# The reciprocal roots of the first two batches on ScalarE and VectorE instead of GpSimd, in a fused attention and Fourier-mixing kernel

## The chip, the core and the metric

The kernel runs on one core of a Trainium2 chip. The core has TensorE (matrix products, the profile's PE, with its weight loads as PEld), VectorE (DVE), ScalarE (ACT), GpSimd (POOL) and SyncE (SP), which here issues every data transfer. Each engine takes its instructions in the order in which they stand in its own queue, and waits for what they need. The metric is device microseconds for one execution, and lower is better. A difference of 0.2%, some 4.3 us here, is about what a measurement of this kernel can tell from no change.

## What is computed

The reference is an attention block, its heads joined to rows of 768, and behind it a mixing block. For 8 batches, 12 heads, 448 tokens and a head dimension of 64:

```python
def rmsnorm(x, g):
    rms = np.sqrt(np.mean(x * x, axis=-1, keepdims=True) + 1e-06)
    return x / rms * g
q_n, k_n = rmsnorm(q, g_q), rmsnorm(k, g_k)
scores = (1 / np.sqrt(64)) * np.matmul(q_n, k_n.transpose(0, 1, 3, 2))
attn = softmax(scores)                      # max taken off, sum + 1e-9
x = heads_joined(np.matmul(attn, v))        # [8, 448, 768]
u = x + real(fft(fft(x, axis=1), axis=2))
un = (u - mean(u)) / np.sqrt(var(u) + 1e-06)
out = u + np.maximum(un @ w_ch1, 0) @ w_ch2 # 768 -> 3072 -> 768
```

The change touches one thing in it: the factor 1/rms of every token and head, for queries and keys, in batches 0 and 1 of the 8.

## The kernel before

**Stages of a batch.** `aux(b)` holds everything of batch b ahead of the feed-forward part: `attention` (pair by pair of heads), then `spectral` (the Fourier mixing as matrix products, the sums u and the second norm). `ffn(b, ...)` holds the feed-forward part: 24 "up" steps of 18 matmuls each (line 910) and 36 "down" steps of 12 each (line 931). `merge` interleaves `ffn(b)` with `aux(b+1)` by a ratio of costs, so that TensorE has feed-forward matmuls to do while ScalarE and VectorE work on the next batch's attention. Ahead of `ffn(0)` nothing of the kind is there: `aux(0)` runs by itself, with the first 14 steps of `aux(1)` mixed into its spectral part.

**A pair of heads.** `load_pair` brings queries and keys of two heads to the tile `raw` (112 tokens by 1024) and the values to `v`. `norm_pair` squares them into `qkn`, sums each row of 64 (`V.tensor_reduce` to `ss`, 112x16), scales the sums, takes the power -1/2, and multiplies `raw` by it into `qkn`. `transpose_pair` turns `qkn` on TensorE (tiles `qk`, line 327), splits the result in two parts for two matmul passes (`QT`, `KD`, and `rounded`, which holds the keys' low parts), `softmax_pair` makes the scores `S` (line 375), their row minimum `mn` on VectorE and the exponential `P` on ScalarE, and `value_pair` turns `P` (tiles `rem` and `pt`) into `T` and `R` and multiplies by the values (`av`). In batches 0 and 1 the division by the row sums is made later, on the result (`divide_pair`: `sums`, `rs`, `rt`, `xT`).

**The norm's engines.** In batches 0 and 1 (`b < EARLY`) the squares are made on ScalarE, in the others on GpSimd. The reduction and the scaling are VectorE's, the power is GpSimd's in all batches: one `tensor_tensor` with `ALU.pow` of `ss` (112x16) against a tile of -0.5.

**The weights.** They come as 64-bit numbers. In the first sweep each block is loaded (`dblw`, in the early part `dblw1e` and `dblw2e`), converted and stored back to memory for the later sweeps. `convert` (lines 711 to 731) takes two instructions of ScalarE, three of VectorE, one addition on GpSimd (line 728, tile `magw`), a cast on ScalarE and a subtraction on VectorE (`w`). Loaded blocks share two buffers, so that a load waits for the GpSimd addition of the block two before it.

**The order.** The program is written in the order of these generators, and a scheduler that works with modelled costs then sets the order of each engine's queue. Each generator's step yields a cost. Buffers are few and shared by tag. So a change in one place gives another order in many queues around it. All transfers are issued from SyncE's one queue.

Of the kernel before, what the change touches and what calls it, by code (L numbers as in the profile page):

```python
# [11 lines left out]
F32 = mybir.dt.float32  # L12
# [3 lines left out]
AF = mybir.ActivationFunctionType  # L16
ALU = mybir.AluOpType
# [5 lines left out]
C = 112  # L23
# [19 lines left out]
EARLY = 2  # L43
# [46 lines left out]
def spectral_block(ctx, tc, q, k, v, g_q, g_k, w1, w2, d1, d2, out, nb=B):  # L90
    nc = tc.nc
# [3 lines left out]
    sb = ctx.enter_context(tc.tile_pool(name="sb", bufs=2))  # L95
# [23 lines left out]
    V, A, G = Recorded(nc.vector), Recorded(nc.scalar), Recorded(nc.gpsimd)  # L119
# [59 lines left out]
    nhalf = cpool.tile([128, 16], F32, name="nhalf")  # L179
# [7 lines left out]
    def load_gains():  # L187
        for i, g in enumerate((g_q, g_k)):
            for h in range(2):
                nc.sync.dma_start(  # L190
                    gains[64 * h : 64 * h + 64, i : i + 1],
                    g.rearrange("(d o) -> d o", o=1),
                )
        V.scalar_tensor_tensor(
            out=gneg, in0=gneg, scalar=-(D**-0.5), in1=gains[:, 1:], op0=ALU.mult,
            op1=ALU.mult,
        )
# [49 lines left out]
    def norm_pair(b, p):  # L247
        raw, vt = loaded.pop((b, p))
        qk = sb.tile([C, 2, NC, 2, D], F32, tag="qk", name=f"qkn{b}_{p}", bufs=1)
        sq = qk.rearrange("t i c h d -> t (i c h) d")  # L250
        flat = raw.rearrange("t i h c d -> t (i h c) d")
        nth = b * NPAIR + p
        if b < EARLY:
            A.activation(sq, flat, AF.Square)
        else:
            G.tensor_tensor(out=sq, in0=flat, in1=flat, op=ALU.mult)
        ss = sb.tile([C, 16], F32, tag="ss", name=f"ss{b}_{p}")
        V.tensor_reduce(ss, sq, axis=AX.X, op=ALU.add)
        V.tensor_scalar(
            out=ss, in0=ss, scalar1=1.0 / D, scalar2=EPS, op0=ALU.mult, op1=ALU.add  # L260
        )
        G.tensor_tensor(out=ss, in0=ss, in1=nhalf[:C], op=ALU.pow)
        for i in range(2):
            V.tensor_tensor(
                out=qk[:, i].rearrange("t c h d -> t h c d"),
                in0=raw[:, i],
                in1=ss[:, 8 * i : 8 * i + 8]
                .rearrange("t (h c) -> t h c", h=2)[:, :, :, None]
                .broadcast_to([C, 2, NC, D]),
                op=ALU.mult,  # L270
            )
        if plain(b, p):
            return qk, vt
        vhl = sb.tile([128, 4, 4, D], F32R, tag="vhl", name=f"vhl{b}_{p}", bufs=1)
        A.copy(vhl[:, :, ::3], vt)
        V.tensor_tensor(
            out=vhl[:, :, 1:3], in0=vt, in1=vhl[:, :, ::3], op=ALU.subtract
        )
        return qk, vhl
# [3 lines left out]
    def plain(b, p):  # L283


        return b * NPAIR + p in PLAIN_PAIRS
# [6 lines left out]
    def transpose_pair(b, p):  # L293

        if b >= nb or (b, p) in ready:
            return
        load_pair(b, p)
        qk, vhl = norm_pair(b, p)
        load_pair(*next_pair(b, p))
        yield 0  # L300
# [665 lines left out]
    def warm():  # L966
# [4 lines left out]
        for _ in range(8):  # L971
            nc.tensor.matmul(o, ident, w, start=True, stop=True)

    load_gains()
    load_pair(0, 0)
    warm()
# [41 lines left out]
```

## Time and profile before

| | us |
|---|---|
| median of 3 runs (2168.72 to 2171.92) | 2169.73 |
| the profiled execution | 2168.48 |
| its span, first to last instruction | 2166.7 |
| TensorE busy with matmuls in the span | 2082.8 (96%) |
| VectorE, ScalarE, GpSimd busy | 1556.7, 1055.5, 342.6 |

Times in a timeline or chain row are counted from the start of the span: start, duration, engine, line, operation, tiles written and read, and in brackets how long the engine stood idle before and what ended that. Line 113 is the helper that records ScalarE's, VectorE's and GpSimd's instructions, so the tile names tell them apart. A row of waits gives the sum, the number of times and the longest. A row of a table by stretch gives, for each engine, its busy time and in brackets its instructions; the column behind POOL is TensorE's granted clock as a share of full speed.

### The profile page before, as it was taken

Reading aid. Unit: us, or ns where it says so; the run is one execution under the profiler, and the core shown is the slowest. Engines: PE = TensorE matmul, PEld = TensorE weight load, DVE = VectorE, ACT = ScalarE, POOL = GpSimd, SP = SyncE. Lnnn points to the kernel's source line nnn. Section 1 sums busy time; section 2 is a strip of 40 time slices with the busy share of each in tenths; the row PEclk is TensorE's granted clock in tenths of the full one; section 3 lists DMA queues with packets and bytes.
Section 4 is the critical chain, followed back from the end, with each engine's and each line's share of the span. In section 5 each row is a group of like instructions: output and inputs, shape, how many; then the busy total and the mean of one; then the engine's idle time right before and its main releaser. Section 6 shows DMA issues by size and latency. Waiting matters only on the chain.

```text
span 2166.7 us, 31325 instructions
## 1 busy us (share of the span) xinstructions
PE 2082.8 (96%) x11224; PEld 1857.7 (86%) x11224; DVE 1556.7 (72%) x3003; ACT 1055.5 (49%) x2258; POOL 342.6 (16%) x196
## 2 busy tenths in 40 slices
PE   7877999899999999999999999999999999999997
PEld 4556777789999999999999999999999999998997
DVE  7888878978785788758786688857787588753122
ACT  7967866455552555435552455425553455422100
POOL 3324434221110111001110111101110011000000
PEclk8988999999999999999999999999999999999999
DMA  5647777677565855667565765658556675449665
GB/s 167 185 131 266 243 262 243 204 236 224 162 174 184 244 173 165 186 200 218 165 174 178 224 194 172 179 183 241 166 173 190 188 219 165 157 157 287 214 211 138
DMA packets 298301, 424.74 MB, mean 196 GB/s; under 512 B 186609, under 2 KB 224482, under 8 KB 298146
## 3 DMA queue, kind: packets, MB, share of 16 engines
q1 hardware_dynamic: 298146, 422.74, 63.8%
q8 instruction: 89, 1.46, 0.3%
q14 instruction: 66, 0.54, 0.1%
HBM read 362.50 MB, written 65.27 MB: 197 GB/s over the span
## 4 chain that ended last, share of the span: by engine, by line
PE 79%; DVE 6%; DMA 6%; ACT 4%; issue 2%; POOL 1%; SPq 0%; DVEq 0%; POOLq 0%; ACTq 0%
PE o L931 29%; PE h L910 28%; PE S L375 6%; PE av L485 4%; DMA dblw<-w 4%; PE pt L473 4%; PE y L590 2%; PE qk L327 1%; DMA w<-w 1%; ACT P L113 1%; PE oT L876 1%; POOL magw L728 1%; PE x L622 1%; DVE qkn L113 1%; PE un L822 1%
## 5 line engine op out<-in xcount | busy, mean ns | idle before, releaser
L931 PE MATMUL o<-hs,w 128*128 128x448 f32 x3456 | 794.8, 372 | 7.0 <-DMA w<-w 2.6
L910 PE MATMUL h<-unT,w 128*128 128x448 f32 x3456 | 778.7, 370 | 4.1 <-ACT unT L113 1.6
L931 PEld LDWEIGHTS o<-hs,w 128*128 128x128 f32 x3456 | 639.5, 189 | 64.5 <-DMA w<-w 4.9
L910 PEld LDWEIGHTS h<-unT,w 128*128 128x128 f32 x3456 | 639.2, 188 | 58.2 <-issue 2.4
L113 ACT ACTIVATE P<-S,mn 112x448 f32<-112x448 f32 x384 | 243.7, 636 | 197.9 <-DVE mn L113 183.9
L113 ACT ACTIVATE hs<-h 128x448 fp32r<-128x448 f32 x192 | 104.3, 543 | 311.6 <-PE h L910 309.7
L113 DVE TENSOR_REDUCE mn<-S 112x1 f32<-112x448 f32 x384 | 233.7, 618 | 28.1 <-PE S L375 25.5
L113 DVE SCALAR_TENSOR_TENSOR hs<-h,hs 128x448 fp32r<-128x448 f32 x192 | 119.4, 622 | 149.2 <-ACT hs L113 147.4
L113 DVE TENSOR_TENSOR acc<-o,acc 128x448 f32<-128x448 f32 x240 | 148.7, 620 | 96.8 <-PE o L931 94.2
L113 POOL TENSOR_TENSOR qkn<-raw 112x1024 f32<-112x1024 f32 x36 | 68.6, 1906 | 697.8 <-PE qk L327 354.8
L113 POOL TENSOR_TENSOR ss<-ss,nhalf 112x16 f32<-112x16 f32 x48 | 144.7, 3014 | 183.2 <-DVE ss L113 164.8
L375 PE MATMUL S<-KD,QT 128*112 128x448 f32 x384 | 152.3, 399 | 16.3 <-ACT KD L113 11.1
L113 ACT CAST T<-pt 128x448 fp32r<-128x448 f32 x216 | 113.1, 533 | 99.8 <-PE pt L473 98.5
L485 PE MATMUL av<-T,vhl 128*128 128x448 f32 x432 | 153.4, 383 | 0.0
L113 DVE TENSOR_TENSOR T<-pt,T 128x448 fp32r<-128x448 f32 x216 | 131.6, 618 | 26.6 <-ACT T L113 25.6
L375 PE MATMUL S<-rounded,QT 128*112 128x448 f32 x384 | 143.2, 375 | 0.4 <-DMA v<-v 0.4
L113 DVE TENSOR_SCALAR P<-P,sm 112x448 f32<-112x448 f32 x288 | 122.5, 463 | 4.1
L473 PE MATMUL pt<-ident,P 112*128 112x112 f32 x864 | 121.8, 259 | 0.0
L473 PEld LDWEIGHTS pt<-ident,P 112*128 112x128 f32 x864 | 102.6, 140 | 15.5
L728 POOL TENSOR_TENSOR magw<-magw,dblw 128x512 uint32<-128x512 uint32 (+1 forms) x46 | 75.4, 1639 | 172.9 <-DVE magw L724 103.1
L113 POOL TENSOR_TENSOR rstd<-st,nhalf 112x1 f32<-112x1 f32 (+2 forms) x32 | 19.6, 612 | 492.3 <-DVE st L113 489.2
L375 PEld LDWEIGHTS S<-KD,QT 128*112 128x112 f32 x384 | 69.2, 181 | 27.9 <-ACT KD L113 13.7
(117 smaller groups left out, 2521.9 us busy)
## 6 DMA issues: line engine op xcount, KB each, us to landing
w<-w SPq DMA_DIRECT2D x192, 768.0 KB, 4.5
w<-w SPq DMA_DIRECT2D x288, 512.0 KB, 4.3
dblw<-w SPq DMA_DIRECT2D x28, 512.0 KB, 5.1
dblw<-w SPq DMA_DIRECT2D x18, 768.0 KB, 5.9
raw<-q SPq DMA_DIRECT2D x96, 112.0 KB, 3.3
raw<-k SPq DMA_DIRECT2D x96, 112.0 KB, 3.7
v<-v SPq DMA_DIRECT2D x96, 96.0 KB, 3.1
u_dram<-u SPq DMA_DIRECT2D x24, 336.0 KB, 3.4
```

Source lines behind the costliest of these rows:

```text
L113: ins = emit(*args, **kwargs)
L327: nc.tensor.transpose(pt[:, c * C : (c + 1) * C], qk[:, i, c].rearrange("t h d -> t (h d)"), ident[:C, :C],)
L375: ins = nc.tensor.matmul(s_, QT[:, h, cs], K[:, h], start=step == 0, stop=step == 1)
L473: nc.tensor.transpose(pt[:, c * C : (c + 1) * C], Pc[c][:, 512 * h + j * 128 : 512 * h + (j + 1) * 128], ident[:C, :C],)
L485: nc.tensor.matmul(av[:, :S], lv, T[:, i], start=(j == 0 and i == 0), stop=False)
L590: nc.tensor.matmul(o, src[:, par, t0 : t0 + n], D1[:, ri, par, cols], start=i != 1, stop=i != 0,)
L622: nc.tensor.transpose(xp[:n, i * 128 : (i + 1) * 128], src[:, 3 * half + i], ident)
L728: behind(nc.gpsimd.tensor_tensor(out=bits, in0=bits, in1=low, op=ALU.add))
L822: nc.tensor.transpose(pt[:, OFFS[i] : OFFS[i] + LENS[i]], uns[i][:, p * 128 : (p + 1) * 128], ident[: LENS[i], : LENS[i]],)
L876: nc.tensor.transpose(op[:n, j * 128 : (j + 1) * 128], accs[b][:, 3 * half + j, t0 : t0 + n], ident,)
L910: pace(nc.tensor.matmul(o, w[:, a, c], unT[c][:, z], start=n == 0, stop=n == 17))
L931: pace(nc.tensor.matmul(o, w[:, a, f], hs[4 * g + f][:, z], start=n == 0, stop=n == 11))
```

## The change

In batches 0 and 1 the power -1/2 of `ss` is no longer taken on GpSimd. ScalarE takes the natural logarithm into a new small tile `y`, then the exponential of -1/2 times that, and the square of the result into a second tile `z`. VectorE makes one Newton step with two instructions: z becomes -1/2 z ss, and ss becomes (z + 3/2) y. Batches 2 to 7 keep GpSimd's power. At the program's start ScalarE's table set that holds both logarithm and exponential is asked for explicitly, ahead of the first loads.

```diff
@@ norm_pair
-        G.tensor_tensor(out=ss, in0=ss, in1=nhalf[:C], op=ALU.pow)
+        if b < EARLY:
+            y, z = (
+                sb.tile([C, 16], F32, tag=tag, name=f"{tag}{b}_{p}") for tag in "yz"
+            )
+            A.activation(y, ss, AF.Ln)
+            A.activation(y, y, AF.Exp, scale=-0.5)
+            A.activation(z, y, AF.Square)
+            V.scalar_tensor_tensor(
+                out=z, in0=z, scalar=-0.5, in1=ss, op0=ALU.mult, op1=ALU.mult
+            )
+            V.scalar_tensor_tensor(
+                out=ss, in0=z, scalar=1.5, in1=y, op0=ALU.add, op1=ALU.mult
+            )
+        else:
+            G.tensor_tensor(out=ss, in0=ss, in1=nhalf[:C], op=ALU.pow)
@@ at the program's start
+    nc.scalar.preload_act_table_set("natural_log_exp_and_others")
     load_gains()
     load_pair(0, 0)
     warm()
```

Twelve GpSimd instructions go (of 48 such powers), and 36 ScalarE and 24 VectorE instructions come. The built program holds one table load in both versions. The scheduler gives another order in all queues up to about the end of `ffn(0)`; behind that, TensorE's last 5092 of 5980 rows stand as before.

Three places show how the queues move. The first is the start of ScalarE's queue. The number behind a tile's name is a buffer's; `qkn_0` is the square of the first pair, and each row's wait is by a semaphore name: DMAHW for a transfer, DVE, PE, Activation for an engine. Before:

```order
L113 ACT_TABLE_LOAD [waits DMAHW2_49,DMAHW3_49,DMAHW1_49]
L113 ACTIVATE qkn_0_136<-raw_0_113 112x1024 [waits DMAHW0_49]
L113 CAST QT_0_156<-qk_0_0_158 64x448 [waits PE_49]
L113 CAST QT_0_156<-qk_0_0_158 64x448
L113 ACTIVATE KD_0_157<-qk_0_1_167,gains 64x448 [waits DMAHW4_49,DVE_49,PE_49]
```

and after:

```order
L988 ACT_TABLE_LOAD
L113 ACTIVATE qkn_0_137<-raw_0_114 112x1024 [waits DMAHW2_49,DMAHW3_49,DMAHW1_49,DMAHW0_49]
L113 ACTIVATE y_0_142<-ss_0_139 112x16 [waits DVE_49]
L113 ACTIVATE y_0_142<-y_0_142 112x16 [waits Activation_49]
L113 ACTIVATE z_0_143<-y_0_142 112x16 [waits Activation_49]
L113 CAST QT_0_163<-qk_0_0_165 64x448 [waits PE_49]
L113 CAST QT_0_163<-qk_0_0_165 64x448
```

The table load no longer waits for the first queries and keys, and the three new instructions stand between the square and the first cast.

The second place is VectorE's queue at the end of batch 0's attention, where the folds of the attention's result (`eo`, `tot`, `xT`) stand among the norm of batch 1's second pair (`ss_1`, `qkn_1`) and a weight conversion (`magw2e`, `w2e`). Before:

```order
L716 TENSOR_SCALAR magw2e_1261<-magw2e_1261 128x512
L113 TENSOR_TENSOR qkn_1_1427<-raw_1_1131,ss_1_1429 112x2x4x64 x2
L113 TENSOR_TENSOR tot_1250<-eo_0_1046,eo_1_1243 128x900
L720 TENSOR_SCALAR magw2e_1261<-magw2e_1261 128x512
L113 SCALAR_TENSOR_TENSOR eo_0_1046<-eo_1_1243,eo_0_1046 128x900
L724 SCALAR_TENSOR_TENSOR magw2e_1261<-dblw2e_1262,magw2e_1261 128x512
L113 TENSOR_TENSOR xT_295<-rt_5_1331,xT_295 128x448
L730 TENSOR_TENSOR w2e_1260<-magw2e_1261,w2e_1260 128x512
L113 TENSOR_TENSOR eo_2_1339<-xT_295 128x449 x2
```

and after:

```order
L730 TENSOR_SCALAR magw2e_1304<-magw2e_1304 128x512
L113 TENSOR_TENSOR tot_1293<-eo_0_1083,eo_1_1286 128x900
L734 TENSOR_SCALAR magw2e_1304<-magw2e_1304 128x512
L113 SCALAR_TENSOR_TENSOR z_1_1476<-z_1_1476,ss_1_1472 112x16
L113 SCALAR_TENSOR_TENSOR eo_0_1083<-eo_1_1286,eo_0_1083 128x900
L738 SCALAR_TENSOR_TENSOR magw2e_1304<-dblw2e_1305,magw2e_1304 128x512
L113 SCALAR_TENSOR_TENSOR ss_1_1472<-z_1_1476,y_1_1475 112x16
L113 TENSOR_TENSOR qkn_1_1470<-raw_1_1174,ss_1_1472 112x2x4x64 x2
L744 TENSOR_TENSOR w2e_1303<-magw2e_1304,w2e_1303 128x512
L113 TENSOR_TENSOR xT_308<-rt_5_1374,xT_308 128x448
L113 TENSOR_TENSOR eo_2_1382<-xT_308 128x449 x2
```

The multiplication `qkn_1` moves from ahead of the folds to behind the conversion's third instruction, and the conversion's last one (`w2e`) now stands ahead of `xT`.

The third place is ScalarE's queue where `ffn(0)` begins: `un` are the normed rows, `unT` the feed-forward input that TensorE turns and ScalarE copies out, `magw_1` and `dblw_1` the conversion of the second "up" block. Before:

```order
L113 ACTIVATE un_1_1582<-u_1_1566,st_1_1567 112x768
L714 ACTIVATE magw_1_1622<-dblw_1_1623 128x768
L715 ACTIVATE dblw_1_1623<-dblw_1_1623 128x768
L113 ACTIVATE un_3_1602<-u_3_1588,st_3_1589 112x768
L113 ACTIVATE u_1_1566,st_1_1567<-un_1_1582 112x768
L113 CAST unT_0_1680<-un_0_1675 128x448
```

and after:

```order
L113 ACTIVATE un_1_1631<-u_1_1615,st_1_1616 112x768
L113 ACTIVATE un_3_1651<-u_3_1637,st_3_1638 112x768
L113 ACTIVATE u_1_1615,st_1_1616<-un_1_1631 112x768
L113 CAST unT_0_1729<-un_0_1724 128x448
L113 CAST unT_1_1737<-un_1_1732 128x448
L113 CAST unT_2_1745<-un_2_1740 128x448
L113 CAST unT_3_1753<-un_3_1748 128x448
L728 ACTIVATE magw_1_1671<-dblw_1_1672 128x768
L729 ACTIVATE dblw_1_1672<-dblw_1_1672 128x768
```

The conversion's two instructions move from ahead of `un_3` to behind the first four `unT`.

## The prediction

> **What bounds the kernel now.** The page's shares of the whole span mix stages, so I read a table by stretch first, then the chain of waits, and the timelines of the three places that the queues' order names.
>
> ```profile
> 25.00:125.00 100.00, 78.33 (x383) 52.63 (x382) 90.18 (x157) 96.61 (x214) 39.51 (x22) 0.95 0.59 174
> 125.00:175.00 50.00, 30.68 (x134) 23.27 (x134) 40.31 (x77) 25.64 (x52) 13.63 (x8) 0.74 0.40 132
> 175.00:460.00 285.00, 265.15 (x1314) 219.39 (x1314) 234.77 (x376) 190.55 (x366) 99.92 (x61) 0.97 0.77 252
> 460.00:2166.70 1706.70, 1691.41 (x9348) 1552.35 (x9346) 1178.13 (x2375) 729.97 (x1606) 182.16 (x96) 1.00 0.63 190
> ```
>
> The columns are TensorE, its weight loads, VectorE, ScalarE, GpSimd. From 460 us on TensorE is 99% busy, the change touches nothing there, and the stretch only shifts. Ahead of it are four different stages: a start of 25 us with one chain; batch 0's attention, 25 to 125 us, where ScalarE is busy 96.61 of 100 us and VectorE 90.18; the folds and the Fourier part, where each engine waits for another; and `ffn(0)` with batch 1's attention and the weights' conversion, TensorE at 93%. All twelve changed norms lie ahead of 290 us. So the question is by how much the end of each of these stages moves.
>
> GpSimd is never near full (39.51 of 100 us). Its power matters only where somebody waits for it. The chain of waits goes through just two of the twelve:
>
> ```profile
> 9.02 2.94 POOL ss L113
> ...
> 123.81 4.57 POOL ss L113
> ```
>
> **The first pair (a gain).** In the start everything hangs on one chain:
>
> ```profile
> 5.05 1.28 ACT L113 ACT_TABLE_LOAD   x1 [5.05 <-DMA raw<-k]
> 6.34 1.06 ACT L113 ACTIVATE qkn<-raw 112x1024 f32<-112x1024 f32 x1
> 7.43 1.22 DVE L113 TENSOR_REDUCE ss<-qkn 112x16 f32<-112x1024 f32 x1 [6.04 <-ACT qkn L113]
> 8.57 0.15 DVE L113 SCALAR_TENSOR_TENSOR gains<-gains 128x1 f32<-128x1 f32 x1
> 8.69 0.17 DVE L113 TENSOR_SCALAR ss<-ss 112x16 f32<-112x16 f32 x1
> 9.02 2.92 POOL L113 TENSOR_TENSOR ss<-ss,nhalf 112x16 f32<-112x16 f32 x1 [6.91 <-DVE ss L113]
> 11.98 1.29 DVE L113 TENSOR_TENSOR qkn<-raw,ss 112x512 f32<-112x512 f32 x2 [3.11 <-POOL ss L113]
> ```
>
> The table load stood behind the keys' arrival; in the new queue it has no wait and runs while the transfers do: 1.28 us off the chain. The bound: `gains` sits between the reduction and the scaling in VectorE's queue and waits for transfers of its own. Its row at 8.57 shows no wait, so they land by then, how much earlier no row shows; at the latest end the scaling could move up by only 0.1 us. I take 1.28, with 0.1 as the low end.
>
> The power with its handovers, from 8.86 to 11.98, takes 3.12 us. For the new chain the trace has no logarithm and no 16-element ScalarE instruction with arithmetic, so I bound it by these:
>
> ```profile
> L113 ACT ACTIVATE P<-S,mn 112x448 f32<-112x448 f32 x96 | 60.9, 639 | 27.6 <-DVE mn L113 27.4
> L113 ACT ACTIVATE qkn<-raw 112x1024 f32<-112x1024 f32 x12 | 12.6, 1049 | 0.0
> L113 ACT COPY xT<-xT 128x1 f32<-128x1 f32 x12 | 2.2, 187 | 2.6 <-DVE xT L113 2.5
> L113 ACT ACTIVATE u<-un 112x768 f32<-112x768 f32 x2 | 1.7, 837 | 0.0
> L113 DVE TENSOR_SCALAR ss<-ss 112x16 f32<-112x16 f32 x14 | 2.3, 166 | 0.1
> ```
>
> The squares of 768 and 1024 elements differ by 212 ns, 0.83 ns an element; that leaves 0.21 us for 16 elements. The exponential with its per-row bias, 639 ns at 448, comes to 0.28 by the same slope, and the copy of one element, 0.19, is the floor. So three instructions take 0.57 to 0.84 us, the two of VectorE 0.33 at 0.166 each, and six handovers at the 0.03 that lies between the square's end (7.40) and the reduction's start some 0.2. That is 1.1 to 1.4 us in place of 3.12: a gain of 1.9. **First pair: −3.2 us**, between −1.8 and −3.6.
>
> Here a rule of the Trainium skill can be weighed. The row: the load took 1.28 us and the square began right behind it, at 6.34. ScalarE: Activation LUTs, section "What ACT_TABLE_LOAD costs", has 1283 ns for the load and 1380 ns for a drain, 2.66 us in all for a switch. The load agrees, the drain does not show at the start; by the page the term would be an estimated −4.6 in place of −3.2.
>
> **The seven norms that follow (a loss).** Pairs 1 to 5 of batch 0 and 0 and 1 of batch 1 are normed by 125 us, where ScalarE is the fullest engine. Its waits in that stretch are few, and none is for GpSimd:
>
> ```profile
> ACT T L113 <- PE pt L442: 0.8, 2, 0.7
> ACT P L113 <- DVE mn L113: 0.6, 2, 0.5
> ACT xT L113 <- PE av L454: 0.5, 1, 0.5
> ```
>
> So there is next to nothing to win from the power's absence, and each new ScalarE instruction lengthens a full queue. What one costs there is less than its duration where the next can start over its tail:
>
> ```profile
> 105.08 0.19 ACT L113 COPY xT<-xT 128x1 f32<-128x1 f32 x1
> 105.18 0.67 ACT L714 ACTIVATE magw2e<-dblw2e 128x512 f32<-128x512 f32 x1
> ```
>
> 0.10 us from start to start. Three a pair cost between 0.30 (all overlapped) and 0.84 (none); I take 0.5, since two of three wait for the one before them, though the new queue mostly puts other work between. Seven pairs: **+3.5 us**, between +2.1 and +5.9. VectorE's two, 0.33 a pair and 2.3 us in all, lie in its 9.8 us of idle time; if that cover were gone too, they would add at most those 2.3.
>
> **The second pair of batch 1 (a gain).** VectorE stood behind the slow power at 123.81, and then behind a conversion:
>
> ```profile
> 128.41 1.71 DVE L113 TENSOR_TENSOR qkn<-raw,ss 112x512 f32<-112x512 f32 x2 [0.54 <-POOL ss L113]
> 132.38 0.68 DVE L724 SCALAR_TENSOR_TENSOR magw2e<-dblw2e,magw2e 128x512 uint32<-128x512 uint32 x1
> 133.47 0.63 DVE L113 TENSOR_TENSOR xT<-rt,xT 128x448 f32<-128x448 f32 x1 [0.41 <-ACT xT L113]
> 135.26 0.69 DVE L730 TENSOR_TENSOR w2e<-magw2e,w2e 128x512 fp32r<-128x512 f32 x1 [1.16 <-ACT w2e L729]
> ```
>
> What waits behind it are the folds, and behind them the Fourier matmuls. In the new order the folds `tot` and `eo_0` go first, so the 0.54 us goes, and `qkn` fills part of the 1.16 us for which VectorE waited for the conversion's GpSimd and ScalarE steps: 1.7 us at most. `xT`, though, waits for ScalarE's copy of TensorE's last product, which no norm moves, and it now stands behind `w2e`. I take **−1.2**, between 0 and −1.7.
>
> **The entry of the feed-forward part.** The order, not the norm itself, moves a conversion:
>
> ```profile
> 173.75 0.94 ACT L113 ACTIVATE un<-u,st 112x768 f32<-112x768 f32 x1 [0.88 <-DVE st L113]
> 174.59 0.90 ACT L714 ACTIVATE magw<-dblw 128x768 f32<-128x768 f32 x1
> 175.38 0.93 ACT L715 ACTIVATE dblw<-dblw 128x768 uint32<-128x768 uint32 x1
> 176.18 0.95 ACT L113 ACTIVATE un<-u,st 112x768 f32<-112x768 f32 x1
> ...
> PE un L822 <- ACT un L113: 5.6, 3, 4.0
> ```
>
> `un_3` and the four `unT` behind it come 1.6 us earlier (174.59 to 176.18), and TensorE was waiting for just that. The price: the conversion starts some 3.5 us later (behind one square and four casts), so its buffer is freed later, and the next block's load with it. Loads bind in this stage:
>
> ```profile
> by line: DMA dblw<-w 29.0%; POOL magw L728 7.2%; issue 6.9%; PE o L931 6.1%; ACT magw L714 4.6%; DVE w L730 4.4%; DVE magw L724 4.3%; DVE magw L716 3.5%; DVE qkn L113 2.8%; ACT dblw L715 2.7%; DVE magw L720 2.4%; DVE eo L113 2.2%; PE y L590
> ```
>
> 29% of the chain from 175 to 460 us is a wait for `dblw`. So −1.6 if TensorE stays the limit, and about +2 (3.5 less the 1.6) if the loads do. I take **−0.5**.
>
> **Batch 1's last four norms.** ScalarE is busy 190.55 of 285 us there, so 12 more instructions (2.5 us at 0.21) lie beside TensorE. GpSimd's four powers go from the queue of the conversions' additions, of which I find one that was held up, by 0.4 us:
>
> ```profile
> 223.24 2.91 POOL L113 TENSOR_TENSOR ss<-ss,nhalf 112x16 f32<-112x16 f32 x1 [1.36 <-DVE ss L113]
> 225.00 0.69 DVE L724 SCALAR_TENSOR_TENSOR magw<-dblw,magw 128x512 uint32<-128x512 uint32 x1
> 226.11 1.33 POOL L728 TENSOR_TENSOR magw<-magw,dblw 128x512 uint32<-128x512 uint32 x1
> ```
>
> I take 0. If TensorE's cover were gone, ScalarE's part would cost the 2.5.
>
> **The sum.** −3.2 + 3.5 − 1.2 − 0.5 = −1.4 us on the profiled execution's 2168.48. That one is 1.25 below the median of the runs; I put the change on the median, 2169.73 − 1.4 = **2168.3 us**, inside the 0.2% (4.3 us) that can't be told from no change.
>
> **The rivals.**
>
> *ScalarE's additions find room.* The chain in the attention stage runs over ScalarE, VectorE and TensorE in turn, so the queue that is fullest need not be the one that sets the end. Then the +3.5 falls to about 0, and with −3.2, −1.7 and −1.6 at the other places the time is 2169.7 − 6.5 = 2163. Against it stands 96.61 of 100. 25%.
>
> *Slower: the new chain is held up in ScalarE's queue.* The power ran on an engine with room. The three new instructions stand apart in a full queue, with casts, exponentials and conversions between them, and VectorE's multiplication waits for the last. If each costs its full 0.28 us, the attention stage grows by 5.9, and if the later conversion at the entry decides, 2 come on top: −3.2 + 5.9 + 2 = +4.7, 2174.5 us. It decides from 0.7 us a pair on. For it: the two fullest engines are those that get the work, and the place of the conversion. Against it: the overlap in the rows above. 22%.
>
> *VectorE itself gets faster without the powers beside it.* This would be contention, and the trace has a case: a subtraction of 128x512 took 1.87 us beside a GpSimd addition, and 0.69 otherwise (135.26 above), 1.2 us lost.
>
> ```profile
> 118.39 1.86 POOL L728 TENSOR_TENSOR magw1e<-magw1e,dblw1e 128x768 uint32<-128x768 uint32 x1 [1.04 <-DVE sums L113]
> 118.92 1.87 DVE L730 TENSOR_TENSOR w2e<-magw2e,w2e 128x512 fp32r<-128x512 f32 x1
> 123.59 0.94 DVE L730 TENSOR_TENSOR w1e<-magw1e,w1e 128x768 fp32r<-128x768 f32 x1
> 189.01 0.95 DVE L730 TENSOR_TENSOR w<-magw,w 128x768 fp32r<-128x768 f32 x1
> ```
>
> Seven powers at 1.2 us would give VectorE 8.4 us back and, with the −1.4, 2160. Against it: the same kind of subtraction of 128x768 began just ahead of the power of 123.81 and ran beside it in 0.94 us, as at 189.01, with no power near, in 0.95. It is the power that is stretched, to 4.57 us. 6%. In the Trainium skill, GPSIMD Engine Reference, section "Architecture", has both engines share read and write ports; by that rule every power would be a competitor, and these rows do not show it for the power.
>
> *It does not do what it says:* if each exponential and logarithm needed its own table, 24 loads of 1.28 us would add 31 us. The built queue holds one load. 2% for this and the like.
>
> **How the numbers follow.** The forecast has 45%, all of it within 0.2%; faster 25 + 6 = 31%; slower 22 + 2 = 24%. The range goes from the contention rival's 2160 to 2176, which is the slower rival with VectorE's 2.3 us half uncovered; beyond lie about 1 in 10 on both sides together, and I leave it there because a new order in all queues has costs that no row bounds.
>
> **What would show it.** The table load ends ahead of 5 us and the first `qkn` multiplication starts near 8.8 in place of 11.98. The three small instructions take 0.19 to 0.28 us each. ScalarE's last `T` of batch 0's attention comes within 3 us of where it was. No idle time of VectorE is put down to the power ahead of 290 us. The first "up" matmul and the end of the first sweep move by the same −1 to −2 us. I am wrong if the stage from 25 to 125 us shortens by 3 us or more, or if `ffn(0)` stretches because its loads start later.

## The result, and the profile after

The changed kernel takes 2180.7 us (median of 4 runs, 2178.2 to 2185.1), where the kernel before takes 2169.25 beside it. The ratio is 1.0054, with a 95% interval of 1.0041 to 1.0066: **slower by 11.5 us**, where 1.4 us faster was forecast and 2176 was the upper end of the range. The profiled execution took 2178.2 us, its span is 2176.4. Lines of `kernel.py` behind the new code count 14 or 15 higher than before: up matmuls L924, down L945, the conversion L728 to L744.

The table by stretch of the changed kernel (TensorE, its weight loads, VectorE, ScalarE, GpSimd, then the granted clock):

```profile
25.00:125.00 100.00, 77.30 (x371) 49.82 (x370) 86.12 (x157) 92.87 (x219) 21.66 (x16) 0.95 0.54 162
125.00:175.00 50.00, 32.59 (x144) 23.60 (x142) 41.93 (x79) 29.71 (x63) 8.45 (x7) 0.80 0.40 127
175.00:460.00 285.00, 260.09 (x1275) 215.32 (x1276) 233.45 (x376) 188.91 (x369) 91.43 (x57) 0.95 0.75 246
```

In the attention stage ScalarE got more instructions and is *less* busy (92.87 for 96.61), and so is VectorE (86.12 for 90.18): the engines wait more for each other. In `ffn(0)` TensorE has 260.09 us of work done where it had 265.15. GpSimd's share falls as meant, from 39.51 to 21.66.

The start of the changed kernel, from the timelines of ScalarE, VectorE and TensorE:

```profile
0.74 1.28 ACT L988 ACT_TABLE_LOAD   x1 [0.74 <-PEq L1016]
...
7.58 0.22 ACT L113 ACTIVATE y<-ss 112x16 f32<-112x16 f32 x1 [1.50 <-DVE ss L113]
7.83 0.22 ACT L113 ACTIVATE y<-y 112x16 f32<-112x16 f32 x1
8.08 0.22 ACT L113 ACTIVATE z<-y 112x16 f32<-112x16 f32 x1
...
8.33 0.17 DVE L113 SCALAR_TENSOR_TENSOR z<-z,ss 112x16 f32<-112x16 f32 x1 [0.78 <-ACT z L113]
...
8.74 1.29 DVE L113 TENSOR_TENSOR qkn<-raw,ss 112x512 f32<-112x512 f32 x2
...
2.16 9.95 PE L986 MATMUL warmed<-warm,ident 128*128 128x512 f32 x16 [2.16 <-POOL ident masks.py:199]
11.95 0.93 PE L341 MATMUL qk<-ident,qkn 112*128 112x112 f32 x8
...
12.53 1.06 ACT L113 CAST QT<-qk 64x448 fp32r<-64x448 f32 x2 [4.24 <-PE qk L341]
```

The chain is what the prediction said: the multiplication starts at 8.74 (8.8 was forecast, 11.98 before). But the transposes `qk` stand in TensorE's queue behind eight dummy products from `warm()`, which end only at 12.1. The first cast moves by 0.9 us, not by 3.2. Before, the warm-up had ended well ahead of the multiplication, and TensorE waited 2.11 us:

```profile
2.16 8.55 PE L972 MATMUL warmed<-warm,ident 128*128 128x512 f32 x16 [2.16 <-POOL ident masks.py:199]
12.81 1.11 PE L327 MATMUL qk<-ident,qkn 112*128 112x112 f32 x8 [2.11 <-DVE qkn L113]
```

From there the shift grows. Each number in this table is the start of one instruction in a run's trace less its start in the trace of before (before's own: 13.43, 25.04, 128.44, 178.50 and 478.48 us). The first two are the first casts `QT` of batch 0's first and second pair; `T` is the last one of batch 0's attention; "up" is the first up matmul of `ffn(0)`; "sweep" is the first up matmul of `ffn(1)`. The last column is the ratio of times to before, with its interval. The rows below the first are the experiments.

| run | QT 1 | QT 2 | last T | up | sweep | ratio |
|---|---|---|---|---|---|---|
| changed kernel | -0.9 | +1.9 | +8.4 | +4.0 | +8.8 | 1.0054 (1.0041 to 1.0066) |
| old_order_control | -0.2 | -0.3 | +0.1 | +0.1 | +2.6 | 0.9998 (0.9989 to 1.0007) |
| new_work_old_order | -1.1 | -0.6 | +6.1 | +6.8 | +8.6 | 1.0034 (1.0021 to 1.0046) |
| no_newton_old_order | -2.2 | -1.9 | -0.3 | -1.0 | -1.2 | 1.0011 (1.0002 to 1.0021) |
| all_pairs_3_warm | -2.8 | -2.4 | +2.2 | +2.1 | +3.4 | 1.0027 (1.0017 to 1.0037) |
| first_pair_3_warm | -3.4 | -3.4 | -3.3 | -2.5 | -4.4 | 0.9992 (0.9983 to 1.0001) |
| first_pair_short_chain | -4.0 | -4.0 | -3.7 | -4.1 | -4.7 | 0.9992 (0.9982 to 1.0001) |
| two_pairs_short_chain | -4.2 | -4.2 | -3.6 | -2.9 | -1.6 | 1.0002 (0.9992 to 1.0011) |
| old_work_new_order | -1.3 | +1.4 | +6.6 | +2.2 | +6.7 | 1.0048 (1.0036 to 1.0061) |
| old_then_new_order | -1.5 | -1.5 | -1.4 | -0.3 | +8.1 | 1.0049 (1.0036 to 1.0062) |
| new_then_old_order | -0.9 | +1.7 | +8.4 | +4.1 | +1.5 | 1.0021 (1.0013 to 1.0030) |
| late_conversion | +0.1 | +0.1 | +0.2 | +1.2 | +2.5 | 1.0025 (1.0016 to 1.0034) |
| early_conversion | -2.0 | +0.8 | +8.7 | +9.6 | +15.9 | 1.0076 (1.0062 to 1.0090) |
| new_transfer_order | -1.2 | -1.3 | -1.1 | +5.7 | +15.2 | 1.0086 (1.0071 to 1.0101) |
| load_and_conversion_back | -0.6 | -0.6 | -0.2 | +0.2 | +5.2 | 1.0029 (1.0017 to 1.0040) |
| before_4_warm | -0.2 | +1.5 | +6.4 | +5.0 | -0.4 | 1.0029 (1.0018 to 1.0041) |
| before_6_warm | +0.4 | +0.4 | +3.6 | +3.4 | +9.0 | 1.0059 (1.0046 to 1.0071) |
| before_7_warm | +0.2 | +1.9 | +6.2 | +3.8 | +0.2 | 1.0014 (1.0006 to 1.0023) |

The control is the kernel before again. It says how far one profile's shift can be trusted: within 0.3 us up to `ffn(0)`, within some 2.5 us behind it, where waits for loads fall differently in each execution. The ratios rest on 4 to 12 runs each; one run of the control took 2736.8 us, some 26% above its others, and is left out of its ratio as slow.

### The profile page after: what moved, and what is told of

It is laid out like the page before. It is cut to its first block, busy times and chain, and to the rows that moved or that the text cites. A ratio compares the mean times of both kernels' runs of the same rounds, so it can differ in the third digit from the quotient of the medians.

```text
span 2176.4 us, 31358 instructions
## 1 busy us (share of the span) xinstructions
PE 2086.2 (96%) x11224; PEld 1856.2 (85%) x11224; DVE 1558.0 (72%) x3027; ACT 1060.4 (49%) x2294; POOL 307.5 (14%) x184
## 4 chain that ended last, share of the span: by engine, by line
PE 80%; DMA 6%; ACT 6%; DVE 5%; POOL 1%; issue 1%; SPq 0%; POOLq 0%; DVEq 0%; ACTq 0%
PE h L924 29%; PE o L945 29%; PE S L389 6%; PE av L499 4%; PE pt L487 4%; DMA dblw<-w 4%; PE y L604 2%; DMA w<-w 1%; PE qk L341 1%; ACT P L113 1%; PE oT L890 1%; ACT KD L113 1%; POOL magw L742 1%; PE x L636 1%; PE ab L677 1%
## 5 line engine op out<-in xcount | busy, mean ns | idle before, releaser
L945 PE MATMUL o<-hs,w 128*128 128x448 f32 x3456 | 795.3, 372 | 9.9 <-DVE w L744 2.6
L924 PE MATMUL h<-unT,w 128*128 128x448 f32 x3456 | 779.7, 371 | 2.4 <-ACT unT L113 1.6
L945 PEld LDWEIGHTS o<-hs,w 128*128 128x128 f32 x3456 | 639.0, 189 | 68.5 <-issue 4.5
L924 PEld LDWEIGHTS h<-unT,w 128*128 128x128 f32 x3456 | 639.9, 189 | 56.1 <-issue 2.6
L113 POOL TENSOR_TENSOR ss<-ss,nhalf 112x16 f32<-112x16 f32 x36 | 106.8, 2967 | 143.1 <-DVE ss L113 129.9
```

Of the source, the lines that this page charges most:

```text
L113: ins = emit(*args, **kwargs)
L924: pace(nc.tensor.matmul(o, w[:, a, c], unT[c][:, z], start=n == 0, stop=n == 17))
L945: pace(nc.tensor.matmul(o, w[:, a, f], hs[4 * g + f][:, z], start=n == 0, stop=n == 11))
```

## The experiments

### Work or order

The change does two things: it adds 60 instructions, and with them the scheduler gives another order in all queues. To part them, each engine's queue was held to a list. Every kernel whose order is held has this at the end of the program (shortened here). The program's own rule that paces the conversions in the early part (each behind the fourth-last instruction of its engine) also sets nothing but an order; it is switched off there, or the new instructions are left out of its count, and in the control it stays:

```diff
+def pin(tc, nc, rows):          # rows: per engine, places in the order of writing
+    ...
+    for engine, runs in rows.items():
+        seq = [mine[engine][k] for a, n in runs for k in range(a, a + n)]
+        for one, two in zip(seq, seq[1:]):
+            tc.add_manual_dep(two, one.name, NoSync, reason="pinned")
```

The edges order instructions on one engine only and add no wait. The rows are before's order or the changed kernel's, read from the built programs. The control holds before's program to before's order.

> The kernel before, unchanged but for the added edges that hold every queue to the order it has anyway: the control for all the runs whose order is held. It should be within 2 us of before, its landmarks up to 477 us within 0.5 us of before's. A second question for its trace: most profiles of the other runs lose 1 to 4 us between 1830 and 1980 us that before's profile does not lose (its 2808th to 3024th up matmul take 140.5 us). If that belongs to the chip and not to a kernel, this one may show it too.

0.9998: holding the order costs nothing. Its trace answers the second question too. Between 1830 and 1980 us it loses 2.0 us against before's profile, at a granted clock of 0.99 for 1.00. The row of the control, by stretch:

```profile
1830.00:1980.00 150.00, 147.69 (x814) 135.61 (x813) 96.37 (x193) 56.28 (x121) 6.98 (x6) 0.99 0.56 181
```

and of before:

```profile
1830.00:1980.00 150.00, 148.00 (x826) 136.15 (x825) 95.30 (x192) 54.35 (x117) 5.09 (x5) 1.00 0.57 183
```

So one program in one order can show that loss in one execution and not in another, and I leave it out of what follows. Whether some versions have it more often is not shown.

The new work in before's order (36 instructions on ScalarE, 24 on VectorE more, 12 on GpSimd fewer, the table load early, every other row of all queues as before):

> The whole change in arithmetic and the early table load, but every engine's queue is held to the order that it had before the change: the new ScalarE instructions stand where GpSimd's power began in the trace of before, the two of VectorE just ahead of each multiplication. Theory 'order': the 11 us are a matter of the new order of the queues, and the added work is small; then the time is within 3 us of before (2166 to 2172), the last T of batch 0 comes within 2 us of before and the first sweep ends within 2 us of where it did. Theory 'work': the 36 and 24 added instructions in ScalarE's and VectorE's full queues cost it; then 2176 or more, with batch 0's last T some 6 to 8 us late. The prediction's own +3.5 for ScalarE would show as the last T 0.3 to 3 us late (+3.5 less the 0.9 that the start gained).

+7.4 us: nearer to "work" than to "order". The old work in the changed kernel's order:

> The converse: GpSimd's power as before (plus the early table load, which moves no queue), and every engine's queue held to the order that it has in the changed kernel, GpSimd's powers put where the changed kernel had the scaled sums ready. Theory 'order': slow as the changed kernel or slower, 2176 to 2186. Theory 'work': as before, within 3 us of 2169. If both this and the first are slow, or both fast, the loss comes from the two together.

+10.4 us, with not one instruction of the new chain. (Of the change it has the early table load; so have the four runs of old work below that mix two orders.) **Both theories hold, and they don't add:** 7.4 and 10.4 by themselves, 11.5 together. I read this as the work's price lying, for the most part, in waits that the new order has already; no run takes that apart.

### What the work costs

The fourth pair's norm in the run with the new work in the old order, from the timelines of ScalarE, VectorE and GpSimd:

```profile
49.23 0.22 ACT L266 ACTIVATE y<-ss 112x16 f32<-112x16 f32 x1
49.48 0.21 ACT L267 ACTIVATE y<-y 112x16 f32<-112x16 f32 x1
49.72 0.21 ACT L268 ACTIVATE z<-y 112x16 f32<-112x16 f32 x1
49.95 0.63 ACT L113 ACTIVATE KD<-qk,gains 64x448 fp32r<-64x448 f32 x1
...
50.61 0.69 DVE L113 SCALAR_TENSOR_TENSOR rounded<-qk,gains,KD 64x448 fp32r<-64x448 f32 x1 [0.99 <-ACT KD L113]
...
53.13 0.46 DVE L269 SCALAR_TENSOR_TENSOR z<-z,ss 112x16 f32<-112x16 f32 x1
53.62 0.52 DVE L272 SCALAR_TENSOR_TENSOR ss<-z,y 112x16 f32<-112x16 f32 x1
54.17 1.29 DVE L113 TENSOR_TENSOR qkn<-raw,ss 112x512 f32<-112x512 f32 x2
...
52.26 1.30 POOL L742 TENSOR_TENSOR magw2e<-magw2e,dblw2e 128x512 uint32<-128x512 uint32 x1 [8.42 <-DVE magw2e L738]
53.50 0.61 POOL L113 COPY rs<-sums 112x512 f32<-112x512 f32 x1
```

The same place before, from VectorE's and GpSimd's timelines:

```profile
50.04 0.69 DVE L113 SCALAR_TENSOR_TENSOR rounded<-qk,gains,KD 64x448 fp32r<-64x448 f32 x1 [0.28 <-ACT KD L113]
...
52.56 1.91 DVE L113 TENSOR_TENSOR qkn<-raw,ss 112x512 f32<-112x512 f32 x2
...
52.03 1.29 POOL L728 TENSOR_TENSOR magw2e<-magw2e,dblw2e 128x512 uint32<-128x512 uint32 x1
```

The three instructions hold ScalarE for 0.72 us (49.23 to 49.95). The scaling of the keys, `KD`, comes that much later, and VectorE's subtraction `rounded` waits 0.99 us for it in place of 0.28: ScalarE's whole 0.7 us arrive at VectorE. Then VectorE spends 1.04 us on its own two (0.41 where nothing runs beside them: 73.88 to 74.29 for the next pair). Not all of the 1.04 is added: here they stand beside GpSimd's addition, which before ran beside the multiplication, and the multiplication takes 1.29 us for 1.91. From the norm's start on VectorE to the multiplication's end the stretch grows from 1.91 to 2.33 us, by 0.42. Over the six pairs between QT 2 and the last T the shift grows from -0.6 to +6.1, **1.1 us a pair**, the sum of the two parts (0.72 and 0.42). The run with 3 warm-up calls has the same order and 0.75 a pair (-2.4 to +2.2). For the test, the square and the Newton step were left out:

```diff
-            A.activation(y, y, AF.Exp, scale=-0.5)
-            A.activation(z, y, AF.Square)
-            V.scalar_tensor_tensor(out=z, ...)
-            V.scalar_tensor_tensor(out=ss, ...)
+            A.activation(ss, y, AF.Exp, scale=-0.5)
```

> All twelve pairs with the logarithm and the exponential alone, in before's order of the queues; the square and VectorE's Newton step are left out (a less exact root). In the run with the whole chain in this order each pair took ScalarE 0.72 us in a row (49.23 to 49.94 for the fourth pair) and VectorE 0.41 just ahead of its multiplication (53.13 begins, 53.62, and 73.88 to 74.29 for the fifth). Theory 'series' (ScalarE's and VectorE's queues wait for each other in turn, so both parts lengthen the path: 1.13 a pair): with 0.47 of ScalarE and nothing of VectorE the shift from the third cast QT to batch 0's last T falls from +6.3 us to 0.47/1.13 of it, 2 to 3.3, and the whole time from 2177.5 to 2171 to 2174. Theory 'ScalarE alone' (VectorE's part is hidden in its idle time, as the prediction had it): the shift falls only by the square's 0.25 a pair, by 1.5 to 2 us in all, and the time is 2175 to 2176.

2170.7 us, +2.4 by the ratio; the shift over the six pairs falls from 6.7 to 1.7 us. "Series" said 2171 to 2174 and 2 to 3.3, and both came out lower by less than half a us; "ScalarE alone" said 2175 to 2176. Series holds, and it holds as well against the 0.75 a pair (4.5 us over the six): there it gives 1.9, and ScalarE alone 3.0. A small instruction on VectorE was not hidden by VectorE's 9.8 idle us. My reading is that each of these idle pieces waits for ScalarE or TensorE, and what follows it waits for VectorE.

Two VectorE instructions of 0.17 us took 0.46 and 0.52 while GpSimd's addition (52.26 to 53.56) and copy (53.50 to 54.11) ran. GPSIMD Engine Reference in the Trainium skill, section "Specifications", has the SBUF interfaces shared with VectorE, with contention for instructions with two SBUF inputs; both VectorE instructions are of that kind, and the rows agree.

### The start

> Queues held to before's order; the new chain only for the very first pair, the power for the other eleven; 3 warm-up matmul calls in place of 8, which leaves out dummy products only. Theory 'floor' (TensorE's warm-up, busy until 12.1 us in the changed kernel, stands ahead of the first transposes and swallowed most of the 3.2 us): the first cast QT comes at 10.0 to 11 us in place of 12.53 and 13.42 before, and the time falls by 2 to 3 us against before, to about 2167. If the floor were something else, the cast stays near 12.5. If the 3 us are lost behind the start all the same (loads bind later), the cast comes early and the time stays within 1 us of before. If fewer warm-up products lower the clock that TensorE is granted, the first scores take longer and part of the gain goes.

```diff
-        if b < EARLY:
+        if nth == 0:
             y, z = (...)
@@ warm
-        for _ in range(8):
+        for _ in range(3):
             nc.tensor.matmul(o, ident, w, start=True, stop=True)
```

The first cast comes at 9.99: the floor was the warm-up. The 3.4 us stay through all of batch 0's attention (-3.3 at its last T) and are -4.4 at the end of the sweep. The whole time shows less: by the ratio -1.7, and in the profile -1.0 at the end, most of the rest lost between 1830 and 1980 us, where the control loses too. The whole change with 3 calls:

> As the kernel with the whole change in before's order, with 3 warm-up calls in place of 8. Against the kernel with the first pair alone it prices the other eleven pairs in one and the same order: theory 'order' within 1 us of it; the prediction's sum (+3.5 for the seven norms of the full stretch, -1.2 for the second pair of batch 1) 2 to 3 us above it; theory 'work' 8 us or more above it.

+5.9 us by the ratio, 7.6 above the run with the first pair alone: near "work". From TensorE's timeline of this run, where the transposes now wait for VectorE again and not for the warm-up:

```profile
2.15 4.67 PE L986 MATMUL warmed<-warm,ident 128*128 128x512 f32 x6 [2.15 <-POOL ident masks.py:199]
9.57 1.73 PE L341 MATMUL qk<-ident,qkn 112*128 112x112 f32 x8 [2.74 <-DVE qkn L113]
```

The first pair without its Newton step, before's order, 3 calls:

> Before's order, 3 warm-up calls, only the first pair on logarithm and exponential (no square, no Newton step for it), the other eleven on GpSimd. The first multiplication should start at 8.1 (8.55 less the square's 0.25 and VectorE's 0.41, plus a handover), the first cast at 9.3 to 9.5, and the first sweep end 0.5 us earlier than with the whole chain for this pair: -4.9 in place of -4.4. Theory 'floor': all of it carries to the end, 2165 to 2167. If the clock that is granted near the end takes it back, as in the profile of the run with the whole chain (-4.4 at 477 us, -0.4 to -1.3 behind 1970 us), 2167 to 2169.

As expected up to the sweep (first cast 9.43, -4.7), and 2166.9 us. This and the run with the first pair's full chain have the lowest medians of the versions tried. Both are faster than the changed kernel by some 13 us; against before, 0.9992 with an interval that just reaches 1, neither is shown to be faster. Doing the same for batch 1's second pair too (`nth in (0, 7)`), where the prediction saw VectorE wait for a power of 4.57 us:

> Before's order, 3 warm-up calls, logarithm and exponential alone for the first pair and for batch 1's second one, where VectorE waited 0.54 us for a power of 4.57; the other ten on GpSimd. Against the run with the first pair alone (first sweep's end -4.3 to -4.6): if the wait for the power was on the path, 0.3 to 0.5 us more, less what 0.47 us of ScalarE costs: within 0.5 us of it, 2164 to 2168.

1.0002, 2169.9 us, where 2164 to 2168 was expected: nothing more is won there. The last T stands where it stood with one pair (-3.6 for -3.7), the up matmul 1.2 us later.

### What the order costs, and where

Before's order up to the entry of `ffn(0)`, the changed kernel's behind it, old work; and the converse:

> GpSimd's powers as before (old work). Every queue stands in before's order up to the entry of ffn(0) (TensorE's first normed rows, ScalarE's un_1), and behind it in the changed kernel's order. The run with old work in the changed kernel's order throughout was 10.4 us slower than before: its entry of ffn(0) came 2.2 us late, its first sweep ended 6.7 us late. Theory 'ffn': the new order loses in ffn(0), some 4.5 us and what follows; then the first sweep ends 4 to 7 us late here and the time is 2174 to 2179. Theory 'attention': the loss is made ahead of the entry and only shows later; then the first sweep ends within 2 us of before and the time is 2168 to 2172.

> The converse: old work, the changed kernel's order up to the entry of ffn(0), before's order behind it. Theory 'ffn': the entry 2 us late and the first sweep's end 2 to 3 us late, 2171 to 2173. Theory 'attention': 6 to 10 us late as with the new order throughout, 2176 to 2181. If this and its converse both come to half, the two parts add up.

+10.6 and +4.6 us. With the new order the loss is in `ffn(0)`: there the entry is on time (-0.3) and the sweep ends 8.1 us late. The attention's new order makes the entry 4.1 us late; the sweep then ends 1.5 us late, the difference being no more than the control's scatter. By the ratio this part costs something by itself (2.8 to 6.5 us), so these two don't add to 10.4 either. In the first of the two runs this is how it looks, first on ScalarE and then on TensorE:

```profile
204.04 0.19 ACT L113 ACTIVATION_READ_ACCUMULATOR P<-S,mn 112x1 f32 x1
207.74 0.89 ACT L714 ACTIVATE magw<-dblw 128x768 f32<-128x768 f32 x1 [3.51 <-DMA dblw<-w]
...
210.81 0.53 ACT L113 COPY T<-pt 128x448 f32<-128x448 f32 x1
...
211.40 1.86 PE L449 MATMUL av<-T,v 128*128 128x448 f32 x2 [3.63 <-ACT T L113]
```

A conversion waits 3.51 us at the head of ScalarE's queue for a block that has not landed; a copy `T` stands behind it; TensorE's `av` waits 3.63 us for `T`; and the fifth up step stands behind `av`. Next the prediction's own place, the second up block's conversion behind `un_3` and `unT_0` to `unT_3` on ScalarE (shown), VectorE and GpSimd, all else in before's order, and its reverse in the changed kernel:

```diff
@@ ScalarE's rows, before -> late_conversion
 un_1
-magw_1
-dblw_1
 un_3
 u_1
 unT_0
 ...
 unT_3
+magw_1
+dblw_1
```

> The kernel before in its own order, but for the block at the entry of ffn(0): un_3 and unT_0 to unT_3 ahead of the conversion of the second up block (magw_1), on ScalarE, VectorE and GpSimd, as the changed kernel has them. This is the prediction's term of -0.5 (between -1.6 and +2) by itself. TensorE-bound: first up matmul 1.6 us earlier and the sweep's end with it. Load-bound: the conversion 3.5 us later (185 in place of 180 for its last cast), third and later blocks late, the sweep's end +2 or more; in the changed kernel the fifth up step (matmul 72) was 13 us late and the entry 4, so if this block does it, matmul 72 comes 5 us or more late here.

> The changed kernel with all its work, in its own order, but for the same block: the conversion of the second up block ahead of un_3 and unT, as before had it. The entry should come 1.6 us later than in the changed kernel. If the late conversion is what makes the fifth up step 13 us late, matmul 72 comes 5 us or more earlier than in the changed kernel (220.4), and the time falls from 2180.7 to 2174 to 2177; if not, the time stays within 2 us of the changed kernel.

The first costs 5.4 us (the third and the fifth up step begin 3.8 us late each; at the fifth the changed kernel is 13 us late, so the block does part of that, not most of it). Its ScalarE shows why nothing is won at the entry:

```profile
178.32 0.84 ACT L113 ACTIVATE u<-un 112x768 f32<-112x768 f32 x1 [1.47 <-DMA u_dram<-u]
...
180.85 0.95 ACT L714 ACTIVATE magw<-dblw 128x768 f32<-128x768 f32 x1
```

Without the conversion ahead of it, ScalarE is held by a row transfer instead: the square behind `un_3` waits 1.47 us for `u_dram`, and the first up matmul comes 1.2 us later, not 1.6 earlier. The conversion itself starts 6.3 us later than before (180.85 for 174.59). The second, expected to mend, makes the changed kernel worse, 1.0076: I had taken the late conversion for the cause, and it is a consequence. The load itself had moved, on a queue that the prediction did not look at. From the timeline of SyncE's queue, before:

```profile
169.00 0.40 SPq L711 DMA_DIRECT2D dblw<-w  x1
...
172.58 0.34 SPq L760 DMA_DIRECT2D w<-w2e  x1
173.05 0.34 SPq L635 DMA_DIRECT2D u_dram<-u  x1
```

The load of the second up block is issued at 169.00. In the changed kernel's order it stands behind the store of `w2e`, which waits for the conversion of the `w2e` block, and behind the row transfer. To price the new order of the transfers, SyncE's queue alone was given it from the entry on, all compute queues keeping before's. That moves some thirty of its 420 rows against the others, most by a few places, the four loads of one pair's queries and keys by some 15; the cut below shows the first of them. And the load and the conversion were both put back in the run with the new order behind the entry:

```diff
@@ SyncE's rows, before -> new_transfer_order
 u_dram<-u_2
-dblw_1<-w
 w_5<-w2e
 u_dram<-u_1
+dblw_1<-w
 dblw_2<-w
```

> Old work, all compute queues in before's order; SyncE's queue of transfers in before's order up to the entry of ffn(0) and behind it in the changed kernel's order, so the load of the second up block stands behind the store of w2e and the row transfer u_dram. Theory 'transfers': its load is issued at about 173 in place of 169.0, ScalarE's conversion, which stands ahead of un_3, waits for it (it did for 6.3 us in the run with the conversion put back), the first up matmul comes 4 to 6 us late and the sweep's end 5 us or more; 2174 or more. Theory 'compute order': the load comes later without a consumer being late for long, the sweep's end within 2 us and the time within 3 us of before.

> Old work, before's order up to the entry of ffn(0) and the changed kernel's behind it (10.6 us slower than before when unmended), but with the load of the second up block and its conversion both back where before has them. If that one block's lateness sets off the rest (buffers freed late, later loads late), the fifth up step (matmul 72), 8.2 us late in the unmended run, comes at least 4 us earlier and the time falls to 2171 to 2174. If the loss lies in what stands further behind, matmul 72 moves by less than 2 us and the time stays at 2176 to 2179.

The transfers' order alone costs **18.6 us**, more than the whole change. At the entry it goes by the path that was expected. From SyncE's, ScalarE's and TensorE's timelines of that run:

```profile
172.03 0.35 SPq L760 DMA_DIRECT2D w<-w2e  x1
172.51 0.34 SPq L635 DMA_DIRECT2D u_dram<-u  x1
172.94 2.10 SPq L711 DMA_DIRECT2D dblw<-w  x2
...
173.20 0.94 ACT L113 ACTIVATE un<-u,st 112x768 f32<-112x768 f32 x1 [0.88 <-DVE st L113]
180.44 0.89 ACT L714 ACTIVATE magw<-dblw 128x768 f32<-128x768 f32 x1 [6.30 <-DMA dblw<-w]
...
182.02 0.92 ACT L113 ACTIVATE un<-u,st 112x768 f32<-112x768 f32 x1
...
182.99 1.01 PE L822 MATMUL un<-ident,un 112*128 112x112 f32 x4 [7.05 <-ACT un L113]
```

The load goes out at 172.94. ScalarE, in before's order, comes to its conversion first and waits 6.30 us; `un_3` stands behind it, and TensorE waits 7.05 us for `un_3`. I read the changed kernel's later conversion as the scheduler's answer to the later load. But this one load is not the 18.6 us. The shift is +5.7 at the first up matmul and only +2.7 at the first down matmul (213.4 us in before); then it jumps to +10.5 by the fifth down step (230 in before) and +15.0 by the eighth (270). The same kind of wait does that again, with another load. From SyncE's timeline before:

```profile
218.38 0.38 SPq L711 DMA_DIRECT2D dblw<-w  x1
219.13 0.91 SPq L231 DMA_DIRECT2D v<-v  x2
```

and from SyncE's, ScalarE's and TensorE's with the new order of transfers:

```profile
221.83 0.91 SPq L231 DMA_DIRECT2D v<-v  x2
...
226.54 0.53 SPq L711 DMA_DIRECT2D dblw<-w  x1
...
230.82 0.65 ACT L715 ACTIVATE dblw<-dblw 128x512 uint32<-128x512 uint32 x1 [5.79 <-DMA dblw<-w]
...
233.33 0.45 PE L430 MATMUL rem<-ident,P 112*128 112x112 f32 x1 [5.17 <-ACT P L113]
```

Here a block's load stands behind the transfers of a pair's values, ahead of which it stood before; ScalarE waits 5.79 us for it and TensorE 5.17 for the `P` behind. No run moves the entry's load by itself.

Putting both back takes 4.3 of the 10.6 us away (1.0049 to 1.0029) and leaves matmul 72 where it was, 8.4 us late: expectation and rival each half right. The rest of `ffn(0)`'s new order holds further such places, of which the wait of 3.51 us (2.95 in this run) is one; they were not taken apart.

### Is before's order a special one?

Three more orders of the old work: the kernel before with 4, 6 and 7 warm-up calls (`range(4)` and so on in `warm`), the scheduler free.

> The kernel before, powers on GpSimd, with 4 warm-up matmul calls in place of 8 (dummy products are left out) and the scheduler free to set every queue again. Nothing waits for the dropped products: in before the first multiplication (11.98) ends behind the warm-up. The scheduler still gives another order in all queues: a probe of what any other order costs. Theory 'the old order is an especially good one': 3 to 10 us slower than before, without any new work. Theory 'the change's order is an especially bad one': within 3 us of before.

> As the one with 4 warm-up calls, with 7: a second draw of an order from the same program and the same work. 'The old order is especially good': 3 to 10 us slower than before; 'the change's order is especially bad': within 3 us of before. One of each would say that orders scatter by some us either way.

> A third draw of an order from before's own work: 6 warm-up calls in place of 8, the scheduler free. 4 calls gave 1.0029, 7 calls 1.0014. 'Before's order is an especially good one': slower than before again, by 2 to 8 us. 'Orders scatter around before's': as likely faster.

+6.3, +3.0 and +12.8 us, for leaving out dummy products that nothing waits for. Each is slower by its ratio; the change's order (+10.4) lies among them. They don't lose at the same place: with 6 calls the 9.0 us are there at the end of the first sweep, with 4 calls that is on time (-0.4) and the next sweep ends 5.9 late, and with 7 calls the trace shows no loss up to 1830 us (+0.2) and 2.7 in the stretch where the control loses 2.0. So before's order is a good one among these, and the change's is an ordinary one. Three draws show the direction, not a distribution.

## Why the prediction was wrong, by its own steps

Two steps weigh most: the new order of the queues, which had no term in the sum and costs 10.4 us by itself, and the seven norms, whose term of +3.5 was a half to two thirds of what they cost in before's order.

- **First pair, -3.2: the chain right, its cover missed.** The multiplication came 3.23 us earlier, the table load ended at 2.02, the small instructions took 0.22 each. The step that failed is "everything hangs on one chain": TensorE's queue held a second one, the warm-up, that ended at 12.1 in the changed kernel. -0.9 in place of -3.2; with 3 calls -3.4 is there and lasts through the first sweep. (The range's end of -3.6 doesn't come out of its own terms: 1.28 and 3.12 less 1.1 make 3.3.)
- **The seven norms, +3.5: right in sign, too small.** Of its two parts ScalarE's was taken as 0.5 a pair with overlap, and is 0.72 in a row; VectorE's was taken as hidden in idle time, and is not (0.42 in the fourth pair, 0.41 in the fifth). In before's order the two come to 1.1 a pair in one run and 0.75 in another, 5 to 8 us for seven. The rival's own threshold, "from 0.7 us a pair on", was passed. That rival, 22%, is the one that came nearest: 2174.5 against 2177.5 for the work alone and 2180.7 for the whole change.
- **The second pair of batch 1, -1.2: not confirmed.** Taking that power away in before's order gave nothing. The term also counted on the folds' new place in VectorE's queue, which that run doesn't have; no run tests it apart.
- **The entry of the feed-forward part, -0.5: wrong.** The reordered conversion alone costs 5.4 us (3.5 to 7.4), not between -1.6 and +2. The gain of 1.6 was a second chain overlooked: a transfer holds the square behind `un_3` as soon as the conversion is out of the way. The delay of 3.5 is 6.3. And the order shown there was ScalarE's only: that the load of that block was moved behind a store in SyncE's queue was overlooked. Where the compute queues don't follow, the first up matmul comes 5.7 us late by way of that load, and SyncE's whole new order costs 18.6. "Wrong if `ffn(0)` stretches because loads start later" is what happened.
- **Batch 1's last four norms, 0: not contradicted.** With the new work in before's order the shift grows by 1.8 us over `ffn(0)`, inside the control's 2.6.
- **The rest of the new order: no term at all.** The sum treated it as the old order plus three moved places. It costs 10.4 us by itself, mostly in `ffn(0)`. The text said that a new order "has costs that no row bounds", and left 1 in 10 for it.
- **The rivals.** Room on ScalarE (2163): no, each added 0.2 us came through. Contention with the power (2160): no sign of a gain. More table loads: one load, as built.

What stays open: how the 11.5 us of the whole change divide between work and order, since the two don't add; why the work costs 1.1 us a pair in one run and 0.75 in another of the same order; which places in `ffn(0)` make up the rest of the order's loss, and in what shares; and what the entry's load costs by itself.

## What to carry to other kernels

Where a scheduler sets the queues, price a change twice: the work by holding the old order, and the order by holding the old work in the new one; a tuned order may be worth more than the change. Ahead of predicting, compare the transfer queue's order first: a load that slips behind a store which waits for compute is late by that wait, and whatever stands behind its consumer is late too. In a stage where engines wait for one another in turn, don't count on a busy share below 100% to hide small instructions: at 90% busy, VectorE's two of 0.17 us came through at 0.41 and 0.42 a pair.

## What was not expected of the hardware

- The eight warm-up calls, identical work, took 8.55 us in one execution and 9.95 in the other, and three calls took 4.67 to 5.49. A floor of this kind moves from run to run.
- Dependent ScalarE instructions on 112x16 start 0.25 us apart at 0.22 us each; logarithm, exponential and square cost the same.
- A VectorE instruction of 112x16 with two inputs took 0.17 us alone and 0.46 and 0.52 beside GpSimd. Both times it ended 0.03 us behind GpSimd's instruction: 53.59 for 53.56, and 54.14 for 54.11.
- One and the same program, in the same order, ended its first sweep at 478.5 us in one profile and at 481.0 in another.
